# Splitting 34-row loads and writing the last tile's spectrum in smaller parts, in a convolution by short transforms

## The chip, the cores and the metric

The kernel runs on one core of one Trainium2 chip. The metric is the device time of one execution in microseconds (us). The kernel before took 275.33 us (median of 6 runs, 274.47 to 278.63).

## The reference

A 7 x 7 circular convolution of an image of 224 x 224 pixels with 96 channels, bf16 in and out, written with Fourier transforms:

```python
wp = jnp.pad(w, ((0, H - K), (0, W - K), (0, 0), (0, 0)))
Xf = jnp.fft.rfft2(x.astype(jnp.float32), axes=(1, 2))
Wf = jnp.fft.rfft2(wp.astype(jnp.float32), axes=(0, 1))
Yf = jnp.einsum('bhwi,hwio->bhwo', Xf, Wf)
y = jnp.fft.irfft2(Yf, s=(H, W), axes=(1, 2)).astype(jnp.bfloat16)
```

## The kernel before, in words

**The method.** The kernel transforms along the rows' direction h only, and in short pieces. The height is cut into 8 blocks `j` of 28 rows (`B`); with 6 rows of overlap a block has `L` = 34 rows, which gives `NS` = 17 frequencies of a real and an imaginary plane (`FR` = 34 planes). Along w the convolution is done directly, with a fast scheme that makes two pixels from fewer products (`TAPS`). The width is cut into `NT` = 7 tiles of 32 pixels; the last one is `TL` = 6.

**The stages of a tile.** (1) `a_jobs` or `f_jobs`: TensorE multiplies pixels (`xn`) by the forward matrix `Fm` into `xf`. (2) `jit`: for a group of three frequencies (`JGB`) VectorE makes the sums and differences of planes, `J`, in three instructions. (3) `b_round`: for each frequency `s`, TensorE multiplies `J` and `xf` by the transformed filters `WF` into two PSUM banks; ScalarE takes one bank into `tt_`, VectorE forms `u` and `v`, and a sum of `v` and `u` gives `yf`. That sum (`ysum`, lines 562 to 573) runs on GpSimd, but on VectorE in the rounds in which the planes of another group are made (`ydve`), and in the last three rounds of the last tile. So in the last tile VectorE sums frequencies 3, 6, 9, 12 and 14 to 16 (frequency 0 has a form of its own, on VectorE too), GpSimd sums 1, 2, 4, 5, 7, 8, 10, 11 and 13. The tiles `u`, `v` and `tt_` have two buffers each, `yf` has four (`YBUF`). (4) When a group of frequencies is complete (`y1`), `yf` is written to a scratch in DRAM (`put`, line 583). (5) `load_t` loads the scratch back with the planes of several blocks on the partitions, and `c_jobs` multiply by the inverse matrix `G`, move the result to `yo` and store it to the output.

**Scratch loads of tiles 0 to 5.** A tile is loaded back in five pieces (`LT`). Four have 112 rows. The piece `gi` = 2 holds blocks 6 and 7, twice: pixels 0 to 11 in loads of 64 and 4 rows, and pixels 12 to 15 in two loads of `FR` = 34 rows each (lines 601 and 602).

**The last tile.** It isn't loaded with `load_t`, and its writes go to a scratch per part. `PARTS` cuts the 17 frequencies into parts; `YGRPL` says the same for `yf`. The parts below `SA` = 9 have the matrix `GA` and two loads each, one for either half of the blocks (`load_p`, lines 616 and 617); those above have `GB` and one load. `GA` and `GB` are filled from `G` by small DMAs, 4 for each part below `SA` and 8 for each above (`g_parts`, 44 in all), one of which is issued in each round of tiles 3 to 5 (line 836). The write of a part goes to GpSimd's queue, and that of the very last to ScalarE's (line 586); it stands right after the round that completes the part, in the order of the program. The loads are issued by SyncE in rounds fixed by hand: three rounds after the part's end, two for the part that ends at 14 (lines 838 to 840); the last two are issued between the remaining jobs of tile 5, behind the loop (lines 846 to 848).

**The end.** After the last round TensorE does the remaining jobs of tile 5, then eight products with `GA` (`first`), 12 filler matmuls into the last of these banks (`WARM`), and then the products with `GB` (`second`), each followed by a move out of PSUM and, for two of them together, a store.

**What sets the order.** Every engine's order is that of the program: the wrapper `_Ordered` ties each instruction to the one before on its engine, and each DMA to the one before among all DMAs. Its line 87 is the line that the profile names for nearly every instruction, so operations are told apart by tile names: `scrl` is the last tile's scratch, `scr` that of the others, `tt` the loaded piece, `xf<-scrl` the load of a part (it lands in the buffer of tile 5's `xf`), and part of the output passes through buffers named `J` and `tt`. SyncE issues nearly all DMAs, one after the other, and waits in that queue for what each needs.

Of the kernel before, what the change touches and what calls it, by code (L numbers as in the profile page):

```python
# [16 lines left out]
NS = L // 2  # L17
# [12 lines left out]
NSLOT = 2 + 3 * (NS - 1)  # L30
PGRP = ((0, 2), (2, 5), (5, 8), (8, 11), (11, 14), (14, 17))
YGRP = ((0, 3), (3, 6), (6, 9), (9, 12), (12, 15), (15, 17))
YGRPL = ((0, 3), (3, 6), (6, 9), (9, 12), (12, 14), (14, 16), (16, 17))
SA = 9
PARTS = (0, 3, 6, 9, 12, 14, 16, 17)
YMAX = 3
YBUF = 4
JGB = ((0, 3), (3, 6), (6, 9), (9, 12), (12, 15), (15, 17))
# [14 lines left out]
def kernel(  # L53
# [7 lines left out]
    _, H, W, C = x.shape  # L61
# [6 lines left out]
    FR = 2 * NS  # L68
# [69 lines left out]
    def dma(out_ap, in_ap):  # L138
        return DE.dma_start(out=out_ap, in_=in_ap)
# [9 lines left out]
    prt = []  # L149
    for a, b in zip(PARTS[:-1], PARTS[1:]):  # L150
        prt.append((a, b, int(a >= SA), (4 if a < SA else NJ) * 2 * (a - (0 if a < SA else SA))))
    assert SA in PARTS and NJ * 2 * (NS - SA) == 128
    XW = 2 * TW * C
# [264 lines left out]
    def a_jobs(t):  # L418
        xf = new_xf(t)
        jobs = []  # L420
        for jg in range(2):
            for h in range(2):
                for (q, n) in ((0, 3), (3, 3), (6, 2)):
                    jobs.extend(a_bank(t, xf, xn_bufs[jg], h * PXC + 2 * q, n, jg, HALO + h * 8 + q))
            jobs.append(then_load(jobs.pop(), t + 1, jg))
        return jobs
# [24 lines left out]
    def jit(t, g):  # L451
        s0, s1 = JGB[g]
        n = s1 - s0
        xf = xf_tiles[t][0:C]
        xv = xf.rearrange("c p r s w j -> c p r s (w j)")
        b = jcount[0] % 3 if t < 2 else (jcount[0] - 2 * len(JGB)) % 2
        jcount[0] += 1
        Jb = J_bufs[b][0:C].rearrange("c (k s q) -> c k s q", k=7, s=3)
        for s in range(s0, s1):
            jbuf[(t, s)] = Jb[:, :, s - s0]  # L460

        def sub(o, i0, i1, op, cost):
            def f():
                load["v"] += 170 + cost * n / 1.92
                return VE.tensor_tensor(out=o, in0=i0, in1=i1, op=op)
            return f
        x0, x1 = xv[:, 0, :, s0:s1], xv[:, 1, :, s0:s1]
        pd, rd, sd, qd = x1.ap
        dpl = bass.AP(x1.tensor, x1.offset - NJ, [pd, [NJ, 2], rd, sd, qd])
        return [  # L470
            sub(Jb[:, 0:4, 0:n].rearrange("c (k r) s q -> c k r s q", r=2), dpl,
                x0.unsqueeze(1).to_broadcast([C, 2, 2, n, PP]), ALU.subtract, 4 * PP),
            sub(Jb[:, 4, 0:n], xv[:, 0, 0, s0:s1], xv[:, 0, 1, s0:s1], ALU.add, PP),
            sub(Jb[:, 5:7, 0:n], Jb[:, 0:4:2, 0:n], Jb[:, 1:4:2, 0:n], ALU.add, 2 * PP),
        ]
# [3 lines left out]
    def b_round(t, s, mid, end, ydve=False, planes=()):  # L479
# [7 lines left out]
        }  # L487
        for (y0, y1) in (YGRPL if t == TL else YGRP):
            if s == y0:
# [87 lines left out]
        if s == y1 - 1:  # L577
            dst, yo0 = scr_tiles[t], 0
            if t == TL:
                i = sum(s >= b for b in PARTS[1:])  # L580
                dst, yo0 = scr_tiles[(t, i)], PARTS[i]

# [8 lines left out]
    def load_t(t, gi, h):  # L591
        tt = t2_pool.tile([128, 12, 2 * C], BF16, name="tt2") if gi == 2 else t_pool.tile([128, 8, 2 * C], BF16, name="tt")
        tt_tiles[(t, gi, h)] = tt
        sv = scr_tiles[t].rearrange("w j s (r e) -> (j s r) w e", r=2)
        if gi < 2:
            dma(tt[0:112, 0:8], sv[gi * 3 * FR:gi * 3 * FR + 112, h * 8:(h + 1) * 8])
        else:
            r0 = 6 * FR
            for p0, p1 in ((0, 64), (64, 2 * FR)):
                dma(tt[p0:p1], sv[r0 + p0:r0 + p1, 0:12])  # L600
            for j in range(2):
                dma(tt[2 * FR:3 * FR, 4 * j:4 * j + 4], sv[r0 + j * FR:r0 + (j + 1) * FR, 12:16])

    TW2 = 2 * TW * C
    tl_all = xf_bufs[(TL + 1) % 2].rearrange("c p r s w j -> c (p r s w j)")
# [3 lines left out]
    def load_p(i):  # L609
        a, b, h, r0 = prt[i]  # L610
        sv = scr_tiles[(TL, i)].rearrange("w j s (r e) -> (j s r) w e", r=2)
        n = 2 * (b - a)
        if h:
            dma(tl_b[r0:r0 + NJ * n], sv)
        else:
            for g in range(2):
                dma(tl_a[g][r0:r0 + 4 * n], sv[g * 4 * n:(g + 1) * 4 * n])

    def g_parts():
        for a, b, h, r0 in prt:  # L620
            n = 2 * (b - a)
            for j in range(NJ if h else 4):
                o = GB[r0 + j * n:r0 + (j + 1) * n, j // 4] if h else GA[r0 + j * n:r0 + (j + 1) * n]
                dma(o[:, j % 4 * B:(j % 4 + 1) * B], G[2 * a:2 * b, 0:B])
                yield
# [59 lines left out]
    def pump():  # L685
        while pend and held[pend[0][1] == 2] < (NTT, 1)[pend[0][1] == 2]:
            held[pend[0][1] == 2] += 1
            load_t(*pend.pop(0))

    def queue_c(t):  # L690
        pend.extend((t, *k) for k in LT)
        pump()
# [35 lines left out]
    def fills(qs, k):  # L728
        def f():
            for q in qs:  # L730
                pace(q, k)
        return f
# [3 lines left out]
    def add(a, b, jobs):  # L736
        qs.append([a, b, jobs, len(jobs)])
# [18 lines left out]
    for r in range(NS + LAG):  # L756
# [31 lines left out]
        for t in range(2):  # L788
            s = r - LAG * t
# [13 lines left out]
    gp = g_parts()  # L803
    for t in range(2, NT):
        if t == TL:
            scr_tiles[t] = None
            for i, (a, b, _, _) in enumerate(prt):
                scr_tiles[(t, i)] = dr_pool.tile([TW, NJ, b - a, 4 * C], BF16, name=f"scrl{i}")
        else:
            scr_tiles[t] = dr_pool.tile([TW, NJ, NS, 4 * C], BF16, name="scr")  # L810
        qs = []
        if t + 1 < NT:
            add(4 if t == 2 else 0, 26, a_jobs(t + 1))
        nold, nnew = CQ[t]
        k1 = 2 * NS if t < TL else 2 * NS - 8
        k0 = 10 if t == 2 else 3
        km = k0 + -(-(k1 - k0) * nold // (nold + nnew))
        if t == TL:
            km = 13
        add(k0, km, cj[:nold])  # L820
        cn = c_jobs(t - 1)
        cj = cn[nnew:]
        add(km, k1, cn[:nnew])
        plan = {}
        for g, (s0, s1) in enumerate(JGB):
            if g + 1 < len(JGB) or t + 1 < NT:
                plan[s0 if g + 1 < len(JGB) else s0 - 1] = g
        for s in range(NS):
            now = ()
            if s in plan:  # L830
                g = plan[s]
                now = jit(t, g + 1) if g + 1 < len(JGB) else jit(t + 1, 0)
            if s == 3:
                queue_c(t - 1)
            if t in (3, 4, 5):
                next(gp, None)
            if t == TL:
                for i, (_, b, _, _) in enumerate(prt[:5]):
                    if s == b + (3 if i < 4 else 2):
                        load_p(i)  # L840
            b_round(t, s, fills(qs, 2 * s), fills(qs, 2 * s + 1), bool(now) or (t == TL and s >= NS - 3), now)
    tail[0] = 2
    assert not pend
    for f in cj[:2]:
        f()
    load_p(5)
    cj[2]()
    load_p(6)
    for f in cj[3:]:
        f()  # L850
    if NP2:
# [61 lines left out]
```

## Time and profile before

| what | value |
|---|---|
| median of 6 runs | 275.33 us |
| lowest, highest | 274.47, 278.63 us |
| the profiled execution | 278.63 us, span 276.9 us |
| TensorE busy | 264.0 us (95% of the span) |
| VectorE, ScalarE, GpSimd busy | 228.3, 196.9, 101.7 us |
| packets of SyncE's queue | 45708, 44.34 MB, 58.8% of 16 engines |
| writes of `scrl` on GpSimd's queue | 6, 0.56 us each (median), 4.7 us to landing (median) |

The span runs from the first to the last instruction of the profiled execution; 1.7 us of its time lie outside. Tiles 0 and 1 share the time up to about 100 us with the preparation of the filters; tiles 2 to 5 follow at about 26 us each; tile 6 has its rounds from about 233 to 260 us, and the end follows. "Busy" of a DMA on GpSimd is the time in which the engine works on its issue. A bracket at the end of a timeline's line gives the idle time of the engine before it and what ended it.

### The profile page before, as it was taken

The numbers are of one execution on the slowest core, as the hardware profiler recorded it, in microseconds if no ns is written. First come the engines' busy times: TensorE is split into PE (matmuls) and PEld (weight loads), VectorE is DVE, ScalarE is ACT, GpSimd is POOL, SyncE is SP. The second block draws the span as 40 slices with busy tenths as digits, with TensorE's granted clock in tenths as the row PEclk, the third lists the DMA queues.
The fourth block names the chain that finished last, engine by engine and source line by source line (L and its number), as shares of the span: only waits on it lengthen the run. The fifth ranks groups of instructions, "written<-read, shape, count | busy, mean of one in ns | idle before, by whom it ended". The sixth has DMA issues, their size and how long they took to land.

```text
span 276.9 us, 12064 instructions
## 1 busy us (share of the span) xinstructions
PE 264.0 (95%) x5088; PEld 241.9 (87%) x5088; DVE 228.3 (82%) x465; ACT 196.9 (71%) x475; POOL 101.7 (37%) x152
## 2 busy tenths in 40 slices
PE   8969999998998999999999999999999999999993
PEld 3549989998998999899999999999999999999762
DVE  5528799999999879977888788678988889989843
ACT  5417797868884566898888869988798875463333
POOL 7720022244544556322422423432152224464300
PEclk9985999999999999999999999999999999999999
DMA  7954204141111169798977569897939672979776
GB/s 184 229 98 135 80 26 128 51 144 45 47 45 45 46 208 249 174 266 236 282 236 185 174 198 273 201 206 205 290 118 200 164 235 96 207 210 236 192 213 199
DMA packets 46355, 46.79 MB, mean 169 GB/s; under 512 B 35306, under 2 KB 38006, under 8 KB 46202
## 3 DMA queue, kind: packets, MB, share of 16 engines
q1 hardware_dynamic: 45708, 44.34, 58.8%
q0 software_dynamic: 448, 1.57, 1.8%
q8 instruction: 40, 0.66, 1.0%
q14 instruction: 15, 0.12, 0.1%
q10 hardware_dynamic: 144, 0.10, 0.1%
HBM read 24.65 MB, written 21.33 MB: 166 GB/s over the span
## 4 chain that ended last, share of the span: by engine, by line
PE 61%; DVE 17%; DMA 10%; issue 5%; POOL 2%; ACT 2%; SPq 1%; DVEq 0%; ACTq 0%
PE pb L87 61%; DVE J L87 7%; DMA wq<-in_w_dram 5%; DMA tt<-scr 5%; DVE WF L87 4%; DVE v L87 3%; POOL yf L87 2%; DVE u L87 2%; DVE yf L87 1%; SPq L87 1%; ACT WF L87 1%; ACT xf L87 1%; DVE yo L87 0%; DVE tt L87 0%; DVEq L908 0%
## 5 line engine op out<-in xcount | busy, mean ns | idle before, releaser
L87 PE MATMUL pb<-WF,J 96*128 96x96 bf16 x2898 | 168.5, 206 | 1.1 <-DVE J L87 0.5
L87 PEld LDWEIGHTS <-J 96*128 96x128 bf16 x2898 | 142.4, 98 | 10.4 <-DVE J L87 1.5
L87 POOL TENSOR_TENSOR yf<-v,u 128x384 bf16<-128x384 f32 x85 | 84.7, 1011 | 144.4 <-issue 89.1
L87 ACT CAST xf<-pb 96x408 bf16<-96x408 f32 (+5 forms) x142 | 66.5, 485 | 7.6 <-PE pb L87 5.5
L87 PE MATMUL pb<-WF,xf 96*128 96x96 bf16 (+1 forms) x952 | 61.8, 207 | 3.3 <-DVE WF L87 2.8
L87 DVE TENSOR_TENSOR J<-xf 96x1824 bf16<-96x1824 bf16 (+1 forms) x84 | 60.3, 757 | 0.1
L87 PEld LDWEIGHTS <-xf 96*128 96x128 bf16 x952 | 47.9, 98 | 4.4 <-issue 3.8
L87 PE MATMUL pb<-Fm,xn 118*128 118x136 bf16 (+4 forms) x576 | 44.4, 203 | 0.0
L87 ACT CAST WF<-pb 96x480 bf16<-96x480 f32 (+1 forms) x60 | 29.7, 554 | 10.2 <-PE pb L87 9.9
L87 PE MATMUL pb<-tt,Gm 102*84 102x384 bf16 (+1 forms) x132 | 33.6, 327 | 0.0
L87 ACT CAST yo<-pb 84x384 bf16<-84x384 f32 (+1 forms) x61 | 26.2, 480 | 5.1 <-PE pb L87 3.2
L87 PEld LDWEIGHTS <-xn 118*128 118x128 bf16 x576 | 29.2, 98 | 0.1
L87 ACT CAST J<-pb 84x384 bf16<-84x384 f32 (+1 forms) x62 | 26.8, 482 | 2.4 <-PE pb L87 2.3
L87 PE MATMUL pb<-wq 98*128 98x120 bf16 (+1 forms) x288 | 23.7, 240 | 2.3 <-DMA wq<-in_w_dram 2.3
L87 DVE TENSOR_TENSOR J<-J 96x912 bf16<-96x912 bf16 (+1 forms) x42 | 25.0, 595 | 0.0
L87 PEld LDWEIGHTS <-wq 98*128 98x128 bf16 x288 | 21.3, 151 | 2.8 <-DMA wq<-in_w_dram 2.8
L87 PE MATMUL pb<-wu 128*128 128x512 bf16 (+3 forms) x70 | 18.2, 388 | 1.1 <-DVE ct L87 1.1
L87 DVE TENSOR_TENSOR WF<-WF 96x960 bf16<-96x960 bf16 x15 | 16.8, 1123 | 0.2
L87 PEld LDWEIGHTS <-wu 128*128 128x128 bf16 (+3 forms) x70 | 7.8, 113 | 8.1 <-issue 2.4
L87 DVE CAST WF<-pb 96x400 bf16<-96x400 f32 (+1 forms) x12 | 7.2, 608 | 8.8 <-PE pb L87 8.4
L87 DVE TENSOR_TENSOR yf<-v,u 128x384 bf16<-128x384 f32 x24 | 13.8, 573 | 0.8
L87 PEld LDWEIGHTS <-Gm 102*84 102x84 bf16 (+1 forms) x132 | 11.5, 117 | 1.7 <-issue 0.6
(393 smaller groups left out, 239.8 us busy)
## 6 DMA issues: line engine op xcount, KB each, us to landing
scr<-yf SPq DMA_DIRECT2D x30, 288.0 KB
xn<-in_x_dram SPq DMA_DIRECT2D x12, 672.0 KB
tt<-scr SPq DMA_DIRECT2D x24, 336.0 KB
out_dram<-yo SPq DMA_DIRECT2D x12, 252.0 KB
out_dram<-J SPq DMA_DIRECT2D x12, 252.0 KB
tt<-scr SPq DMA_DIRECT2D x6, 288.0 KB
wq<-in_w_dram SPq DMA_DIRECT2D x1, 1719.0 KB
WF<-in_x_dram SPq DMA_DIRECT2D x2, 672.0 KB
```

Source lines behind the costliest of these rows:

```text
L87: r = fn(*a, **k)
```

## The change

The two loads of 34 rows become two of 32 rows and two of 2 rows, in each of tiles 0 to 5. In the last tile the parts (0, 3), (3, 6), (6, 9) become (0, 2), (2, 4), (4, 6), (6, 8), (8, 9): five writes instead of three on GpSimd's queue, ten loads instead of six, and 52 small fills of `GA` and `GB` instead of 44, so that the last is issued at the end of tile 5. The loads of the parts are issued by the same rule, three rounds after each part's end. The instructions of TensorE, VectorE and ScalarE and their order are the same as before; GpSimd's queue has two more writes, and two of its five early writes now stand between two sums (after frequency 1 ahead of the sum of 2, and after frequency 7 ahead of the sum of 8); SyncE's queue has 24 more issues.

```diff
-YGRPL = ((0, 3), (3, 6), (6, 9), (9, 12), (12, 14), (14, 16), (16, 17))
+YGRPL = ((0, 2), (2, 4), (4, 6), (6, 8), (8, 9), (9, 12), (12, 14), (14, 16), (16, 17))
 SA = 9
-PARTS = (0, 3, 6, 9, 12, 14, 16, 17)
+PARTS = (0, 2, 4, 6, 8, 9, 12, 14, 16, 17)
...
-            for j in range(2):
-                dma(tt[2 * FR:3 * FR, 4 * j:4 * j + 4], sv[r0 + j * FR:r0 + (j + 1) * FR, 12:16])
+            for p0, p1 in ((0, 32), (32, FR)):
+                for j in range(2):
+                    dma(tt[2 * FR + p0:2 * FR + p1, 4 * j:4 * j + 4], sv[r0 + j * FR + p0:r0 + j * FR + p1, 12:16])
...
             if t in (3, 4, 5):
                 next(gp, None)
+                if (t, s) == (5, NS - 1):
+                    for _ in gp:
+                        pass
             if t == TL:
-                for i, (_, b, _, _) in enumerate(prt[:5]):
-                    if s == b + (3 if i < 4 else 2):
+                for i, (_, b, _, _) in enumerate(prt[:7]):
+                    if s == b + (3 if i < 6 else 2):
                         load_p(i)
...
-    load_p(5)
+    load_p(7)
     cj[2]()
-    load_p(6)
+    load_p(8)
```

## The prediction

> **What bounds the kernel now.** I read, in this order, the busy times by stretch, the timeline of the last tile, TensorE's waits, SyncE's queue, and the timeline of the tail. PE is TensorE, PEld its weight loads, DVE VectorE, ACT ScalarE, POOL GpSimd, SPq SyncE's queue. Times are us from the start of the span.
>
> Busy times by stretch (length, PE, PEld, DVE, ACT, POOL, clock, DMA share, GB/s):
>
> ```profile
> 200.00:225.00 25.00, 25.00 (x497) 23.43 (x495) 21.51 (x46) 21.74 (x56) 9.70 (x10) 1.00 0.70 185
> 225.00:240.00 15.00, 15.00 (x314) 13.99 (x313) 14.39 (x30) 9.14 (x23) 5.56 (x7) 1.00 0.51 151
> 240.00:250.00 10.00, 9.95 (x212) 9.32 (x210) 9.15 (x21) 5.24 (x13) 5.04 (x7) 1.00 0.92 212
> 250.00:260.00 10.00, 9.80 (x192) 9.15 (x189) 9.38 (x20) 3.29 (x8) 4.28 (x6) 1.00 0.84 224
> ```
>
> From tile 2 on PE has no room: 25.00 of 25.00 us. Nothing that only moves data sooner can shorten that. The chain of waits gives "DMA tt<-scr" 4.9%, but I don't believe it: the stretch so named, 243.36 to 248.72, is one in which PE works, and TensorE's waits name no DMA after the filters' load at 18 us. In tile 6 (from about 233 us) DVE is as full as PE, and small PE gaps begin. The timeline there (start, length):
>
> ```profile
> 237.17 1.96 POOL L87 TENSOR_TENSOR yf<-v,u 128x384 bf16<-128x384 f32 x2 [2.67 <-issue]
> ...
> 239.05 0.56 DVE L87 TENSOR_TENSOR yf<-v,u 128x384 bf16<-128x384 f32 x1
> ...
> 239.43 0.81 POOL L87 DMA_DIRECT2D scrl<-yf  x1 [0.31 <-POOL yf L87]
> ...
> 239.53 1.40 DVE L87 TENSOR_TENSOR J<-xf 96x1824 bf16<-96x1824 bf16 x2
> ...
> 242.29 1.96 POOL L87 TENSOR_TENSOR yf<-v,u 128x384 bf16<-128x384 f32 x2 [2.05 <-DVE v L87]
> ...
> 244.56 0.56 POOL L87 DMA_DIRECT2D scrl<-yf  x1 [0.31 <-POOL yf L87]
> ...
> 246.11 0.20 PEld L87 LDWEIGHTS <-J 96*128 96x128 bf16 x4 [0.20 <-DVE J L87]
> ...
> 247.42 1.95 POOL L87 TENSOR_TENSOR yf<-v,u 128x384 bf16<-128x384 f32 x2 [2.31 <-DVE v L87]
> ...
> 249.29 0.56 DVE L87 TENSOR_TENSOR yf<-v,u 128x384 bf16<-128x384 f32 x1
> ...
> 249.66 0.56 POOL L87 DMA_DIRECT2D scrl<-yf  x1 [0.30 <-POOL yf L87]
> 249.77 1.40 DVE L87 TENSOR_TENSOR J<-xf 96x1824 bf16<-96x1824 bf16 x2
> ...
> 251.23 0.20 PEld L87 LDWEIGHTS <-J 96*128 96x128 bf16 x4 [0.19 <-DVE J L87]
> ```
>
> Three frequencies make a cycle of 5.12 us (DVE's yf at 239.05, 244.18, 249.29). In it DVE sums one frequency and then makes the planes J for the next three; POOL sums the other two back to back and then issues the part's write. PE, two frequencies ahead, waits for the second of the plane instructions: 251.17, then its weight load at 251.23. That wait is only 0.2 us, but it means that DVE has no slack here: what delays the planes delays PE one for one. The two POOL sums end (239.13, 249.37) just before DVE's burst.
>
> What happens when they do not end before it is also in the trace. The same two-operand sum on DVE beside a POOL sum, and alone:
>
> ```profile
> 257.11 0.99 POOL L87 TENSOR_TENSOR yf<-v,u 128x384 bf16<-128x384 f32 x1 [1.77 <-DVE v L87]
> 257.51 1.01 DVE L87 TENSOR_TENSOR yf<-v,tt__7337 128x384 bf16<-128x384 f32 x1
> ...
> 259.24 0.56 DVE L87 TENSOR_TENSOR yf<-v,tt__7378 128x384 bf16<-128x384 f32 x1
> ```
>
> And the planes, 1.40 above, at the start of tile 5:
>
> ```profile
> 200.70 1.96 POOL L87 TENSOR_TENSOR yf<-v,u 128x384 bf16<-128x384 f32 x2 [3.14 <-issue]
> ...
> 201.83 2.10 DVE L87 TENSOR_TENSOR J<-xf 96x1824 bf16<-96x1824 bf16 x2
> ```
>
> The first lost 0.45 us in 0.59 of overlap, the second 0.70 in 0.83: DVE loses the overlap less about 0.14.
>
> **What the Trainium skill says.** "SBUF — State Buffer", section "Who interferes with whom": a VectorE instruction with two SBUF inputs and a GpSimd one that reads SBUF exclude each other, for the whole instruction of the one that came first. The losses above agree. "Perfetto Trace Analysis", section "DMA Instruction — SWDGE (GPSIMD)": the slice of a POOL-issued DMA is the making of its descriptors, not the transfer. The trace agrees: 0.56 us of POOL, and 4.7 to the landing (median). "DMA: Bandwidth & Descriptors", section "Why a DMA increments its semaphore by 16 and not by 1": a transfer runs on the largest number of DMA engines up to 16 that divides its row count, so 34 rows run on 2, 24 on 12, 32 and 16 on 16, 8 on 8. The trace agrees: the 34-row load issued at 239.79 shows two late semaphore updates, 245.21 and 246.76, and a 24-row load twelve.
>
> **The change part by part.** *Loads of 34 rows.* Two more DMAs in each of six tiles, 12 issues. The two heavily loaded DMA engines are relieved; a load that took 7 to 8 us should take some 3 (the 112-row one issued at 236.47 landed at 241.60, 5.1 us; a 16-row one in the tail took 3.0). Who gains: the jobs on that tile, which already find their data, since no PE wait names them. Value: 0. Were the cover gone, an issue would cost 0.33 to 0.7 us. Bounds: no more than the PE gaps of tiles 2 to 5 could be won (starts of matmuls against their usual step: 1.0 us between 103 and 114, 0.7 between 120 and 236, each beside a DVE burst); a loss needs SyncE to be the last to arrive, and it waits 77.8 us for POOL's sums.
>
> *Small copies of the output matrix.* 12 + 32 = 44 become 20 + 32 = 52; eight more issues of about 0.6 us on SyncE's queue, spread over tiles 3 to 5 ahead of writes of scratch and stores. The last now falls at the end of tile 5, where SyncE waits anyway (230.00 to 234.9 on sums). Value 0.
>
> *Loads of the parts.* Ten instead of six for the first nine frequencies, four more issues, and SyncE's waits for a part's write come at frequencies 5, 7, 9, 11 and 12 instead of 6, 9 and 12. Behind them stand stores of finished rows: the store issued at 252.63 would move behind the wait for frequencies 6 and 7, by about 2.5 us. Its buffer is written again at 263.5, so that is hidden, until it slips by over 5 us.
>
> *The writes on POOL: here I see the price.* Five writes instead of three. Each is 0.31 (wait for POOL's own sum) + 0.56 = 0.87 us of POOL. After frequencies 4-5 and 9-11 the write stands where it stood. Those after 2-3 and 8 follow both sums and have 2 us of idle POOL. But the write of 0-1 now stands between the sums of 1 and 2, and that of 6-7 between the sums of 7 and 8. The sum of 2 starts at 238.16 + 0.87 = 239.03 instead of 238.16, that of 8 at 248.40 + 0.87 = 249.27 instead of 248.40. DVE's burst begins at 239.05 and at 249.29. The whole sum, 0.98 us, falls on it: 0.98 - 0.14 = 0.84 lost, twice: 1.68 us. Should DVE hold POOL off instead, the sum ends after the burst (241.5 + 1.0), and POOL's next sum, which releases DVE at 243.32, starts about 1 us late: the same price. Low end 0 (POOL ready early), high end 1.1 each. All of it passes to PE, because of the wait at 246.11 and 251.23, and PE's work from 256 to 268 follows with breaks of 0.4 us at most.
>
> *The tail.* Twelve filler matmuls bridge the last load:
>
> ```profile
> 266.10 2.12 PE L87 MATMUL pb<-wu 128*112 128x384 bf16 x12
> ...
> 268.19 0.99 PE L87 MATMUL pb<-xf,GB 128*112 128x384 bf16 x5
> ```
>
> They start every 0.163 us, so the next could start at 268.05; it starts at 268.19. The last load (issued at 265.13) landed at 268.10. So earlier landing, from evener loads ahead of it, gives 0.14 us and no more: filler takes its place.
>
> Sum: 12 + 8 + 4 issues at 0, +1.68, -0.14 = +1.5 us. The profiled execution, 278.63 (span 276.9 and 1.7 around it), would become 280.2. It was the longest of six; against their median of 275.33 the same +1.5 gives 276.8, and I take that, on the ground that the page's clock row is below 9 tenths only in slices 3 and 4 (14 to 28 us), before any changed instruction.
>
> **The rivals.** *One collision only* (+0.84 - 0.14 = +0.7, 276.0): one of the two sums slips through, if POOL leaves its DMA sooner than the slice shows. For: at 249.27 against 249.29 hundredths decide who is first; against: either order costs. *Covered* (this one is not slower): PE's distance of two frequencies grows where the loss falls, so that the planes are not missed; then only the tail's gain stays, -0.14, 275.2. For: the burst at 201.83 lost 0.70 and PE had no gap. Against: there PE has the next tile's transforms to do, in tile 6 it has none; it decides if PE's gap at 241 stays under 0.3. *Relief of the DMA engines counts* (faster): the writes of scratch no longer stuck behind slow loads (SyncE's eight loads from 102.29 take 11.86 us) let DVE's buffers come free, and the gaps between 103 and 114 (about 1.0) and the tail's 0.14 go, perhaps 0.2 elsewhere: -1.3, 274.0. Against: each gap is next to a plane burst. *SyncE's queue becomes late* (slower still): the store behind two part waits frees its buffer late and ACT waits; +1 on top, 277.8. *That it does not do what it says* (32 rows no more spread than 34) leaves the time as the writes make it.
>
> **The numbers.** Two collisions 0.55 (own range 276.2 to 277.5), one 0.13, covered 0.15, relief 0.08, queue 0.09. Slower by over 0.5% means over 276.7 (0.5% is about what a measurement of this kernel can tell from no change): two thirds of the first case and all of the last, 0.37 + 0.09 = 0.46. Faster: 0.08 and a little of the covered case, 0.10. Within: 0.44. The range leaves out the relief and half of the last case, and allows the covered one 0.4 for the uncertainty of a median of such runs: 274.8 to 277.8.
>
> **What would show it.** Right: POOL's sums of 2 and 8 start near 239.0 and 249.3 (249.3 plus the first loss); the DVE burst of yf and planes grows from 1.9 to 2.7 us twice; PE gaps of about 1.0 us near 241 and 252; the 34-row loads' issue shrinks; the filler ends without a gap. Wrong: bursts as long as before, or longer with no PE gap, or a PE wait that names a load.

## The result and the profile after

The changed kernel takes 278.14 us (median of 36 runs, 276.35 to 280.61), the kernel before 275.76 (73 runs): ratio 1.0095, 95% interval 1.0079 to 1.0111, or 2.2 to 3.1 us more. The forecast was 276.8 us: slower by 1.5 us, through two collisions between GpSimd's sums and VectorE's bursts. Both are there, one of them larger than forecast, and the measured time lies above the range of 274.8 to 277.8. The ratio leaves out executions more than 1.5% slower than the fastest of their kernel, so it isn't the quotient of the medians; both profiled executions (spans 276.9 and 279.5 us) are such, with a granted clock of 0.74 between 10 and 30 us and of 1.00 from 30 to 276 us in either.

The busy times by stretch, after (columns as in the prediction):

```profile
200.00:225.00 25.00, 25.00 (x501) 23.48 (x499) 21.63 (x46) 21.76 (x56) 9.38 (x10) 1.00 0.69 183
225.00:240.00 15.00, 15.00 (x312) 13.94 (x310) 14.28 (x29) 9.11 (x24) 5.52 (x7) 1.00 0.54 156
240.00:250.00 10.00, 8.81 (x185) 8.18 (x183) 9.18 (x19) 4.90 (x13) 4.70 (x6) 1.00 1.14 251
250.00:260.00 10.00, 8.94 (x191) 8.42 (x189) 9.51 (x20) 3.55 (x9) 5.20 (x7) 1.00 0.72 183
```

Up to 240 us PE is as full as before; in the two stretches of the last tile PE's 9.95 and 9.80 have become 8.81 and 8.94. The granted clock stays at 1.00 in spite of the gaps. Who is late is seen in the timeline of the last tile, after:

```profile
238.79 0.81 POOL L87 DMA_DIRECT2D scrl<-yf  x1 [0.31 <-POOL yf L87]
...
239.37 1.70 DVE L87 TENSOR_TENSOR yf<-v,u 128x384 bf16<-128x384 f32 x1
...
239.63 1.01 POOL L87 TENSOR_TENSOR yf<-v,u 128x384 bf16<-128x384 f32 x1
...
240.99 1.40 DVE L87 TENSOR_TENSOR J<-xf 96x1824 bf16<-96x1824 bf16 x2
...
242.44 0.20 PEld L87 LDWEIGHTS <-J 96*128 96x128 bf16 x4 [1.28 <-DVE J L87]
...
247.57 0.20 PEld L87 LDWEIGHTS <-J 96*128 96x128 bf16 x4 [0.20 <-DVE J L87]
...
250.17 0.56 POOL L87 DMA_DIRECT2D scrl<-yf  x1 [0.30 <-POOL yf L87]
...
250.75 1.01 POOL L87 TENSOR_TENSOR yf<-v,u 128x384 bf16<-128x384 f32 x1
250.76 1.42 DVE L87 TENSOR_TENSOR yf<-v,u 128x384 bf16<-128x384 f32 x1
...
252.11 1.40 DVE L87 TENSOR_TENSOR J<-xf 96x1824 bf16<-96x1824 bf16 x2
...
253.56 0.20 PEld L87 LDWEIGHTS <-J 96*128 96x128 bf16 x4 [1.06 <-DVE J L87]
```

The write of frequencies 0-1 (238.79) and that of 6-7 (250.17) now hold POOL in front of a sum. That sum runs beside DVE's own, which takes 1.70 and 1.42 us instead of 0.56. The planes J come late by as much, and PEld waits 1.28 and 1.06 us for them; before, its waits for planes here were 0.2 us at most. The untouched burst between them (247.57) still costs 0.20.

The chain of work that ended last, after, in order of time (start, length):

```profile
237.48 1.01 POOL yf L87
239.37 1.70 DVE yf L87
241.07 1.09 DVE J L87 x2
...
248.88 1.00 POOL yf L87
250.76 1.42 DVE yf L87
252.18 1.09 DVE J L87 x2
```

It runs through both lengthened sums, but names neither the writes nor POOL's sums of 2 and 8 (239.63, 250.75). DVE waits for no semaphore there: a collision shows only as a longer duration, and has to be found by putting the lines of both engines side by side.

In the tail, after:

```profile
266.55 0.33 SPq L87 DMA_DIRECT2D xf<-scrl  x1
...
267.48 0.33 SPq L87 DMA_DIRECT2D xf<-scrl  x1
...
268.42 2.12 PE L87 MATMUL pb<-wu 128*112 128x384 bf16 x12
...
270.54 0.99 PE L87 MATMUL pb<-xf,GB 128*112 128x384 bf16 x5
```

The GB products follow 2.12 us after the start of the filler, before 2.09: nothing was gained there.

To place the whole difference I took the start of the same matmul in both traces (all 5088 are recorded in each, in the same order) and compared the steps between them. Before / after, in us: start of the run up to a matmul near 97 us, 97.61 / 97.89; from there to the first burst, equal within 0.04; the step with the first burst 7.30 / 8.45; with the second 7.37 / 8.24; from there to the first GA product 11.70 / 11.70; to the first GB product 3.39 / 3.41; to the last matmul 3.95 / 3.95; from there to the end 4.78 / 5.04. The sum is 0.28 + 0.03 + 1.15 + 0.87 + 0.02 + 0.26 = 2.61 us, the whole difference of the spans. "First step", "second step" and "tail" (first GA to first GB product) below are these. Other profiles below have the same two steps: 8.45 and 8.25 with the parts alone, 7.31 and 7.38 with the two writes moved.

### The profile page after: what moved, and what is told of

Its sections match the earlier page's. It is cut to its first block, busy times and chain, and to the rows that moved or that the text cites. A ratio compares the mean times of both kernels' runs of the same rounds, so it can differ in the third digit from the quotient of the medians.

```text
span 279.5 us, 12112 instructions
## 1 busy us (share of the span) xinstructions
PE 263.9 (94%) x5088; PEld 241.7 (86%) x5088; DVE 230.5 (82%) x465; ACT 196.9 (70%) x475; POOL 101.9 (36%) x154
## 4 chain that ended last, share of the span: by engine, by line
PE 56%; DVE 21%; DMA 8%; issue 6%; POOL 3%; ACT 2%; SPq 1%; DVEq 0%; ACTq 0%
PE pb L87 56%; DVE J L87 8%; DMA wq<-in_w_dram 5%; DVE WF L87 4%; DVE v L87 4%; DMA tt<-scr 3%; POOL yf L87 3%; DVE yf L87 2%; DVE u L87 2%; SPq L87 1%; ACT WF L87 1%; ACT xf L87 1%; DVE yo L87 0%; DVE tt L87 0%; DVEq L912 0%
## 5 line engine op out<-in xcount | busy, mean ns | idle before, releaser
L87 POOL TENSOR_TENSOR yf<-v,u 128x384 bf16<-128x384 f32 x85 | 83.8, 1000 | 144.9 <-issue 90.2
L87 DVE TENSOR_TENSOR yf<-v,u 128x384 bf16<-128x384 f32 x24 | 15.8, 657 | 0.8
```

Of the source, the lines that this page charges most:

```text
L87: r = fn(*a, **k)
```

## The experiments

Each ratio is against the kernel before, run on the same chip.

**The loads alone.** The kernel before with only the 34-row loads split:

```diff
-            for j in range(2):
-                dma(tt[2 * FR:3 * FR, 4 * j:4 * j + 4], sv[r0 + j * FR:r0 + (j + 1) * FR, 12:16])
+            for p0, p1 in ((0, 32), (32, FR)):
+                for j in range(2):
+                    dma(tt[2 * FR + p0:2 * FR + p1, 4 * j:4 * j + 4], sv[r0 + j * FR + p0:r0 + j * FR + p1, 12:16])
```

> The kernel before with the 34-row loads split into 32 and 2 rows, nothing else. Collision theory (the two writes that stand between two GpSimd sums cost it all): no change, within 0.3 us of before, no VectorE burst of tile 6 longer than 2.0 us, all gaps of TensorE as before; SyncE's issue of the tt loads gets shorter. Transfer theory (the split loads and SyncE's longer queue cost): at least 0.5 us slower than before, with TensorE or VectorE waiting for a load. Relief theory: 0.3 us or more faster.

Measured: 1.0029 (1.0003 to 1.0055). The steps are those of before, 7.31 and 7.37; the tail is 3.54. What the split does to SyncE is seen in the last group of tile loads, before and then in the changed kernel:

```profile
236.47 8.79 SPq L87 DMA_DIRECT2D tt<-scr  x7
```

```profile
236.79 5.54 SPq L87 DMA_DIRECT2D tt<-scr  x9
```

Nine loads are issued in less time than seven were. It isn't so in every group, but over all tile loads the issues take 35 to 37 us in the five profiles with whole loads and 30 to 33 in the eight with split ones. The transfers are shorter too: in the group shown the two 34-row loads landed 7.0 and 8.0 us after their issue, with two late updates of their semaphore each, and the two 32-row loads after 5.1 and 4.8 us, with sixteen (the forecast had some 3 us). PE gains nothing from it. The trace of the loads alone has one break of its own: from 105.9 to 107.1 us PE stands still in front of a product that takes pixels (`xn`), and the trace names no releaser:

```profile
107.10 0.22 PE L87 MATMUL pb<-Fm,xn 118*128 118x136 bf16 x1 [1.20 <-issue]
```

It makes the way from the matmul near 97 us to the first burst 141.76 us; in all other profiles it is 140.8 to 140.9. Seven of those are of kernels with the same split loads, so I don't put it down to the split. Whether it belongs to the 0.29% stays open. A gain lies outside the interval.

**The parts alone.** The changed kernel with whole 34-row loads (the diff above taken back).

> The changed kernel with the 34-row loads left whole: only the smaller parts. Collision theory: the whole loss, +2.0 to +2.6 us against before, with two VectorE bursts lengthened by 1.1 and 0.9 us and gaps of TensorE of 1.3 and 1.1 us. Transfer theory: clearly less than the changed kernel's +2.6 us, by what the loads cost.

Measured: 1.0106 (1.0067 to 1.0145); first step 8.45, second 8.25. The loss comes with the parts.

**One write at a time.** First with frequencies 6 to 8 in one part, so that only the write of 0-1 stands between two sums (`YGRPL` and the numbers of the loads follow):

```diff
-PARTS = (0, 2, 4, 6, 8, 9, 12, 14, 16, 17)
+PARTS = (0, 2, 4, 6, 9, 12, 14, 16, 17)
```

> The changed kernel with the last tile's first nine frequencies in parts of 2, 2, 2 and 3: only the write of frequencies 0 and 1 still stands between two sums. Collision theory: +1.1 to +1.4 us against before; one long VectorE burst (sum of frequency 3), one gap of TensorE of 1.3 us, the other 0.2 as before. If the small parts cost by their number (8 instead of 9): +2.3 us.

Then with 0 to 2 and 3 to 5 in one part each, so that only the write of 6-7 does (the same follows):

```diff
-PARTS = (0, 2, 4, 6, 8, 9, 12, 14, 16, 17)
+PARTS = (0, 3, 6, 8, 9, 12, 14, 16, 17)
```

> The changed kernel with the first nine frequencies in parts of 3, 3, 2 and 1: only the write of frequencies 6 and 7 still stands between two sums. Collision theory: +0.8 to +1.2 us against before; one long VectorE burst (sum of frequency 9), one gap of TensorE of about 1.1 us; together with the run with the first only it adds up to the whole. If the cost goes by the number of parts: +2.3 us.

Measured: 1.0031 (1.0004 to 1.0059) and 1.0019 (0.9992 to 1.0047). In the traces the first has steps of 8.45 and 7.38, the second of 7.31 and 8.25. Each write has its own price, 1.15 and 0.87 us, and together they make the 2.02 of the change. The two medians are too near to each other to show which costs more; the traces show it.

**All parts, the two writes behind the next sum.** Everything of the change stays, but the writes of 0-1 and 6-7 are issued after GpSimd's sums of 2 and 8:

```diff
+        for f in late_put:
+            f(GE)
+        late_put.clear()
         if s == y1 - 1:
...
+            if t == TL and y1 in (2, 8):
+                late_put.append(put)
+            else:
+                put(DE if t < TL else SE if y1 == NS else GE)
```

> The changed kernel with the same parts, loads and number of writes, but the writes of frequencies 0-1 and 6-7 are issued after GpSimd's next sum (of 2 and of 8) instead of ahead of it. Collision theory: the loss is gone, within 0.5 us of before, both VectorE bursts back at 1.9 us, TensorE's two gaps back at 0.2. Transfer theory (more writes, more loads, later landings): as slow as the changed kernel or slower, since the writes come later still.

Measured: 1.0018 (0.9991 to 1.0045); steps 7.31 and 7.38. The two bursts of that trace:

```profile
234.54 0.56 DVE L87 TENSOR_TENSOR yf<-v,u 128x384 bf16<-128x384 f32 x1
234.56 0.81 POOL L87 DMA_DIRECT2D scrl<-yf  x1
...
244.79 0.56 DVE L87 TENSOR_TENSOR yf<-v,u 128x384 bf16<-128x384 f32 x1
244.82 1.10 POOL L87 DMA_DIRECT2D scrl<-yf  x2
```

The same writes beside the same DVE sums cost DVE nothing: not the DMA's making is the collision, but the sum that it pushes. In the measured time too: 1.0095 less 1.0018 is 0.77%, or 2.1 us, give or take 0.9, where the two steps give 2.02. And the 24 additional issues together cost at most 0.45% of the time.

**The first POOL DMA earlier.** In the trace of before the write of the first part has a slice of 0.81 us, the later ones 0.56. If that belongs to the first DMA that POOL issues, an earlier one takes it over:

```diff
+            put(GE if (t, y1) == (TL - 1, NS) else DE if t < TL else SE if y1 == NS else GE)
```

> The changed kernel, with the last write of tile 5 issued by GpSimd instead of SyncE, so that the write of frequencies 0-1 isn't GpSimd's first DMA of the program. It asks why the first collision took 1.14 us of VectorE and the second 0.86. If the first DMA's longer slice (0.81 against 0.56 us) is a cost of first use and the sum behind it is late by that much: the write of 0-1 takes 0.56, the first burst loses 0.86 like the second, TensorE's first gap falls from 1.3 to about 1.05, the time by 0.25 us. If the difference lies in the place (the write beside VectorE's work): nothing changes.

Measured: 1.0044 (1.0015 to 1.0073); first step 8.13, second 8.24. The first burst of that trace:

```profile
233.53 0.56 POOL L87 DMA_DIRECT2D scrl<-yf  x1 [0.31 <-POOL yf L87]
234.11 1.01 POOL L87 TENSOR_TENSOR yf<-v,u 128x384 bf16<-128x384 f32 x1
234.11 1.44 DVE L87 TENSOR_TENSOR yf<-v,u 128x384 bf16<-128x384 f32 x1
```

The first write of the last tile now has 0.56, DVE's sum 1.44, and the first step is 0.32 shorter. The slice became shorter by 0.25, and the two steps' losses are now 0.83 and 0.87: the collisions differed by the first DMA's longer slice.

**The pushed sums on VectorE.** The sums of 2 and 8 go to VectorE, which makes them alone:

```diff
-            b_round(t, s, fills(qs, 2 * s), fills(qs, 2 * s + 1), bool(now) or (t == TL and s >= NS - 3), now)
+            b_round(t, s, fills(qs, 2 * s), fills(qs, 2 * s + 1), bool(now) or (t == TL and (s >= NS - 3 or s in (2, 8))), now)
```

> The changed kernel with the sums of frequencies 2 and 8 on VectorE instead of GpSimd; the writes stay where they are. Collision theory: no sum of GpSimd falls on a VectorE burst; VectorE pays 0.56 us of its own work twice in place of 1.14 and 0.86, so about 0.9 us faster than the changed kernel and about 1.1 slower than before. If the write itself (its descriptors, its transfer) held VectorE up: the long sums stay and the time is longer than the changed kernel's.

Measured: 1.0019 (0.9986 to 1.0053); steps 7.59 and 7.86, so +0.29 and +0.49 where I had expected about 0.56 each. The trace shows why. Before, DVE stood idle ahead of its next `u`; now its additional sum lies in that gap (before, then this run):

```profile
238.20 0.36 DVE L87 SCALAR_TENSOR_TENSOR u<-pb,tt__6807 128x192 f32<-128x192 f32 x1 [0.44 <-ACT J L87]
```

```profile
235.64 1.00 POOL L87 TENSOR_TENSOR yf<-v,u 128x384 bf16<-128x384 f32 x1 [2.68 <-issue]
...
236.27 0.78 DVE L87 TENSOR_TENSOR yf<-v,u 128x384 bf16<-128x384 f32 x1
...
236.97 0.34 DVE L87 SCALAR_TENSOR_TENSOR u<-pb,tt__6829 128x192 f32<-128x192 f32 x1
```

The additional sum itself runs beside POOL's sum of 1 and takes 0.78 us instead of 0.56, but DVE's burst behind it is no longer lengthened.

**Filler in the place of the DMA.** The kernel before, with two fills of a tile on GpSimd (0.99 us together) between the sums of 1 and 2 and of 7 and 8:

```diff
+    filler = cpool.tile([128, 800], BF16, name="filler")
...
                 y = ysum(GE)
+                if t == TL and s in (1, 7):
+                    GE.memset(filler[:], 0.0)
+                    GE.memset(filler[:, 0:100], 0.0)
```

> The kernel before with its own parts and loads, and two fills of an unused tile (800 and 100 elements, about 0.93 us by the slope between the fills of GA and GB) on GpSimd between the sums of 1 and 2 and between those of 7 and 8. No write, load or transfer is added. Collision theory: the same two lengthened bursts, each by 0.8 to 0.9 us, two gaps of TensorE of about 1.05 us in place of 0.2, +1.7 us against before. Transfer theory: as before.

Measured: 1.0107 (1.0059 to 1.0156), from four executions only; steps 8.10 and 8.18, +0.80 and +0.81. Their 1.6 us lie at the lower end of the interval (1.6 to 4.3 us). The first burst of that trace:

```profile
236.41 0.56 DVE L87 TENSOR_TENSOR yf<-v,u 128x384 bf16<-128x384 f32 x1
236.43 1.40 POOL L87 TENSOR_TENSOR yf<-v,u 128x384 bf16<-128x384 f32 x1
...
236.88 2.21 DVE L87 TENSOR_TENSOR J<-xf 96x1824 bf16<-96x1824 bf16 x2
```

No transfer, no queue and no semaphore of a DMA is added here, and the loss is there all the same. It falls in another place: DVE's sum keeps its 0.56, POOL's takes 1.40, and the planes take 2.21 instead of 1.40.

**VectorE's order turned.** If POOL's sum and DVE's burst cost what they overlap, the planes should go first, and DVE's own sum behind them. The kernel before, in the last tile only:

```diff
-            if ydve and not whole:
+            if ydve and not whole and t < TL:
...
+            if ydve and not whole and t == TL:
+                ysum(VE)
```

> The kernel before, with VectorE's order changed in the last tile alone: the planes J of the next group ahead of VectorE's own sum of that round, instead of behind it. It asks whether TensorE in the last tile really hangs on the planes, as the price of the collisions assumes. If so: its four gaps of 0.15 to 0.3 us next to the bursts go or shrink, 0.4 to 0.8 us faster in the stretch of tile 6. If TensorE hangs on the sum or on something else: no change in these gaps.

Measured: 0.9979 (0.9948 to 1.0011). Steps 7.11 and 6.90, tail 3.25. Repeated:

> The same edit as the run with the planes ahead of VectorE's own sum, measured once more with more runs, since its interval reached from 0.9948 to 1.0011. If the 0.87 us that its trace gained in the steps of the last tile and in the tail are real and the other differences are scatter, the ratio comes out near 1 - 0.87/275.3 = 0.997, with an interval that ends below 1.000. If the planes' order gains nothing that lasts to the end, the ratio comes out between 0.999 and 1.001. In the trace the two steps around the plane bursts should again be about 7.1 and 6.9 us.

Measured: 0.9977 (0.9939 to 1.0014). Steps 7.10 and 6.92, but the tail 3.96. Two medians lie 0.2% below before, and neither interval excludes no change. In the second trace the tail gave back 0.57 of the 0.71 us that the steps up to it had gained:

```profile
261.35 0.33 SPq L87 DMA_DIRECT2D xf<-scrl  x1
...
261.71 2.12 PE L87 MATMUL pb<-wu 128*112 128x384 bf16 x12
...
264.37 0.99 PE L87 MATMUL pb<-xf,GB 128*112 128x384 bf16 x5 [0.54 <-issue]
```

The last load was issued 0.36 us before the filler began, in the first trace 1.30. SyncE had waited in front of it for the write of 14-15 to land: 4.2 us there, 3.3 in the first trace.

**Both.** Writes behind the next sum and planes first:

> The changed kernel with the two writes behind the next sum and the planes ahead of VectorE's own sum in the last tile. If the collisions are the whole loss and the gaps by the planes the only other one in tile 6: 0.4 to 0.8 us faster than before in tile 6, 0.14 more if the last load lands ahead of the filler's end. If VectorE's cycle as such sets the pace: as before.

Measured: 1.0027 (0.9998 to 1.0055). Steps 7.10 and 7.22, tail 4.79. About half of the steps' gain is there (0.35 us, with planes first alone 0.65), and the tail takes more than that: the write of 12-13 took 5.0 us to land (2.7 and 3.0 where planes went first alone), SyncE waited for it, and issued the last load after the filler had begun:

```profile
262.75 2.12 PE L87 MATMUL pb<-wu 128*112 128x384 bf16 x12
...
263.30 0.33 SPq L87 DMA_DIRECT2D xf<-scrl  x1
...
266.24 0.99 PE L87 MATMUL pb<-xf,GB 128*112 128x384 bf16 x5 [1.38 <-DMA xf<-scrl]
```

No version ran that is shown to beat both kernels.

## Why the prediction was right in kind and too small

The case that the prediction thought likeliest, two collisions, came true, but the time is 1.34 us over the forecast.

**The bound: right.** PE is full up to the last tile, and there DVE's burst has no slack. A loss of 1.14 us in DVE's sum (1.70 - 0.56) became 1.15 in PE's step, one of 0.86 became 0.87.

**Which sums, and when: right.** The sum of 8 starts 0.01 us from DVE's (250.75 and 250.76), as forecast (249.27 and 249.29); that of 2 starts 0.26 us behind DVE's instead of just ahead of it, for the reason given below. That the price is POOL's sum itself follows from the run with the writes behind it (no loss) and from the filler (the loss without a DMA).

**The size of the second collision: right.** Forecast 0.84, measured 0.87.

**The size of the first: the step that failed.** Forecast 0.84, at most 1.1; measured 1.15. "Each is 0.31 + 0.56 = 0.87 us of POOL" took the median slice for a write whose own line, shown in the prediction's first timeline, has 0.81. With it the sum of 2 starts not at 239.03 but at 238.16 + 0.31 + 0.81 = 239.28 in before's times. The prediction then had a second fault: "either order costs", and about the same. With the sum starting 0.23 us after DVE's, DVE would have kept something of its head start if the first to start went on. It kept nothing: in all three collisions shown DVE's sum ended 0.42 or 0.43 us after POOL's (241.07 and 240.64; 252.18 and 251.76; 235.55 and 235.12 with the early DMA). So the loss is when POOL's sum ends, plus 0.43, less when DVE's would have ended: 238.16 + 0.31 + 0.81 + 1.01 + 0.43 - (239.05 + 0.56) = 1.11. Measured 1.15, and 0.83 where the slice was 0.56. The two collisions are thus 2.02 us instead of 1.68, and of these 0.34 us the first makes 0.31.

**The loads' issues, the fills of GA and GB, the part loads at 0: not contradicted.** Between the matmul near 97 us and the last one no step but the two bursts changed by more than 0.04 us. The change without the collisions takes 0.18% (-0.09 to 0.45) more than before, so up to 1.2 us could hide in what the steps don't show.

**The tail's gain of 0.14: the second step that failed.** The tail went from 3.39 to 3.41, 0.16 us off the forecast. In four other profiles with split loads it was 3.25 (the 0.14 won), in three 3.54 to 4.79; with whole loads it went from 3.25 to 3.96. The forecast asked only when the last load lands. But its issue (267.48, 0.94 us before the filler) stands in SyncE's queue behind loads that wait for the writes of 12-13 and 14-15 to land. The write of 12-13 took 4.0 us in the changed kernel and 2.3 before, and over all profiles the two took 2.2 to 5.0 us with no pattern that I could tie to the split.

**The rest of the 1.34 us.** With these two terms put right the forecast would have been 275.33 + 2.02 + 0.02 = 277.37 us. Of the 0.77 us still missing, 0.43 is the start: 275.33 was the median of 6 runs, and the 73 runs of before have 275.76. The last 0.34 has no place that the runs show.

**What is left of the traces' difference.** 0.26 us after the last matmul and 0.28 before 97 us. Over all profiles the first varied from 4.6 to 5.4 us and the second from 92.2 to 97.9, so neither is put down to the change. That the two traces differ by just the 2.6 us that the ratio of 1.0095 gives is partly luck: 2.02 is shown, and what the interval of 2.2 to 3.1 us has beyond that is not settled.

**The rivals.** Covered: fallen, since PE's gaps at 241 and 252 are 1.3 and 1.1 us. One collision only: fallen, each was measured alone. Relief of the DMA engines: the relief is real (the issues of the group shown take 5.54 instead of 8.79 us), but no gain of time came with it: 1.0029 alone. SyncE's queue late: SyncE does wait more on the last tile's writes (12.6 us in all, before 7.3), but the kernel with the same loads and the two writes moved, where it waits 9.7, has steps of 7.31 and 7.38. That the split does not do what it says: fallen, by the sixteen updates of a 32-row load.

## What to carry to other kernels

A write issued by an engine that also computes costs more than its slice: ask which instruction stands behind it in the queue, and what that will run beside. Take the duration from that very write's line in the trace, not from a median over the group, and note that the first was longer here. When the middle of a kernel gets faster, the last load does not start earlier by itself; look at what its issue waits for before counting the gain.

## What the runs showed of the hardware

- The first DMA that GpSimd issued had a slice of 0.81 us, all later ones 0.54 to 0.56. It went with the first, whether that was the last tile's first write or, in one run, a write of tile 5.
- Which of two such sums waits isn't told by the recorded starts alone. The Trainium skill, "SBUF — State Buffer", section "Who interferes with whom", says that issue order decides who blocks. The filler run agrees: DVE started 0.02 us first and kept its 0.56, while POOL's sum took 1.40. Behind a DMA, by the recorded starts, it does not: DVE started 0.26 us ahead of POOL's sum and lost 1.14 us, and the same in the runs with the parts alone and with the first write only. Why wasn't settled; the DMA's making alone slowed no DVE sum (0.56 at 234.54 above, beside a slice of 0.81).
- The same section says that a GpSimd instruction that only writes does not contend with a VectorE instruction of two SBUF inputs. No run here tests it: the fills end where DVE's burst begins.
